# Splitting the K and V streams of a decode attention kernel over two DMA queues

## The chip, the cores and the metric

The kernel runs on one core of one Trainium2 chip. The metric is the device time of one execution in microseconds. A "span" is the time from the first to the last instruction in the profile of one execution; it is usually some 2 us less than the time. All ratios below are the mean time of one kernel's fast runs over that of the other's fast runs from the same rounds on the same chip, so they are not quite the ratio of the medians that are quoted.

## The reference, cut to what matters

Two independent problems, A and B, of one decode step of attention with a sliding window. Each has a batch of 2, 32 query heads, 16 key/value heads, and uses the last 4096 positions of a cache.

```python
q = (x @ wq).reshape(B, 1, 32, 128).transpose(0, 2, 1, 3)
k = jnp.repeat(k_cache[:, :, Sk - 4096:, :], 2, axis=1)
v = jnp.repeat(v_cache[:, :, Sk - 4096:, :], 2, axis=1)
p = softmax(jnp.einsum("bhqd,bhkd->bhqk", q, k) * 128 ** -0.5)
o = jnp.einsum("bhqk,bhkd->bhqd", p, v)
out = o.transpose(0, 2, 1, 3).reshape(B, 1, 4096) @ wo
# the results of A and B are concatenated
```

Nearly all of the work is to read K and V once: 2 problems x 16 heads x (K and V) x 2 MB, 134 MB, plus 19 MB of weights.

## The kernel before

A step t handles one "slab": the 4096 keys of one key/value head for both batch entries, 128 partitions x 8192 bf16, 2048 KB. There are 32 K slabs and 32 V slabs. PE is the matrix engine, DVE the vector engine and ACT the scalar engine; SP only issues transfers here. K and V slabs share a ring of eight slots. In step t the kernel

- transposes K(t) on DVE in two halves (X) and multiplies it with the query on PE (S);
- every fourth step, runs a softmax chain for four slabs: maximum on DVE, a few tiny matmuls, the bias copy and the exponentials on ACT, a transpose of the probabilities on DVE, the sum, and the copy of its reciprocal on ACT (rsb);
- multiplies the probabilities with V(t-5) on PE (PV), normalises the result on DVE, and every fourth step (in the last group every step) adds it into the output projection with wo.

K runs five steps ahead of V, since a chain needs the scores of four slabs. Each engine has a fixed list of operations in program order, and waits on semaphores for the others. The order of the loads is also a fixed list, all of it issued from the SP queue:

```python
stream = []
for t in range(NSLAB + LAG):               # NSLAB = 32, LAG = 5
    if t < NSLAB:
        stream.append(("K", t))
    if t >= LAG:
        i = t - LAG
        if i % 4 == 0:
            stream.append(("W", i // 4))   # a piece of wo
        stream.append(("V", i))
# ... slots are dealt out in this order, modulo 8 ...

def issue(key):
    # ... a slot's load waits for the last reader of what was in it:
    # K(t) for X(t-4), V(i) for PV(i-4); W(G) for the projection of group G-2
    stream_dma[key] = dma_op("sp", ring_sem[r], 1,
        lambda e: e.dma_start(ring[:, r, :], src).then_inc(ring_sem[r], 16), deps, "%s%d" % key)

def ensure(key):
    while key not in stream_dma:
        issue(stream[pos[0]])
        pos[0] += 1
```

K and V alternate in this list, so each already has four slots of the ring in the steady state: K the odd ones, V the even ones. At the end, with no K left, V(27), V(29) and V(31) go into slots that K had used. V(31) is loaded in two parts, three quarters and one quarter.

```python
for t in range(NSLAB + LAG + 1):
    i = t - LAG
    if t < NSLAB:
        make_X(t, 0); make_S(t, 0)         # calls ensure(("K", t))
    # ... if t % 4 == 0: first part of the softmax chain (the exponentials are on ACT)
    # ... norm and projection of V(i - 1)
    if t < NSLAB:
        make_X(t, 1); make_S(t, 1)
    # ... if t % 4 == 0: second part of the chain
    if 0 <= i < NSLAB:
        make_PV(i)                         # calls ensure(("V", i))
    # ... if t % 4 == 0: third part of the chain (rsb on ACT)
```

## Time and profile before

| | before |
|---|---|
| time, median of the first 3 runs | 370.98 us (370.94 to 371.55) |
| span of the profiled run | 369.0 us |
| DMA traffic | 153 MB, mean 416 GB/s |
| busy PE / DVE / ACT | 68% / 50% / 6% of the span |

First, lines of the profile's page. The rows "DMA" and "GB/s" cut the span into 40 equal slices; a digit is the mean busy share of the 16 DMA engines in tenths (9 is 90% or more). The q1 line is the SP queue: packets, MB, and the share of the 16 engines' time. The last line sums the chain of work that ended last by engine.

```profile
DMA  8999999999999999999999999999999999999992
GB/s 320 448 414 426 426 425 433 428 426 426 429 424 424 426 423 435 424 428 426 423 431 424 426 426 427 430 425 428 420 430 428 427 423 426 428 424 420 424 418 121
...
q1 hardware_dynamic: 11700, 153.10, 98.0%
...
DMA 87%; DVE 10%; PE 2%; SPq 1%; issue 0%
```

The DMA engines never rest between the first slice and the last one. At 426 GB/s a slab takes 4.9 us, and a K slab and a V slab together 9.8 us. The kernel is bound by the DMA stream.

From the same page, the DMA issues: tensor, queue, count, size of each, and the median time from issue to landing.

```profile
ring<-in_A_k_cache_dram SPq DMA_DIRECT2D x16, 2048.0 KB, 33.8
ring<-in_A_v_cache_dram SPq DMA_DIRECT2D x16, 2048.0 KB, 36.3
```

A slab lands 33 to 36 us after its issue although it only needs 4.9 us of transfer: about seven slabs are queued at any time.

Next, the start of the run in order of time, DVE alone: start, duration, line, operation, and in brackets the idle time before it and what ended it. "x2" merges the two halves of one K slab.

```profile
36.45 4.50 DVE L392 STREAM_TRANSPOSE xt<-ring 128x2048 f32<-128x2048 f32 x2 [0.39 <-DMA ring<-in_A_k_cache_dram]
41.33 4.50 DVE L392 STREAM_TRANSPOSE xt<-ring 128x2048 f32<-128x2048 f32 x2 [0.38 <-DMA ring<-in_A_k_cache_dram]
46.22 4.50 DVE L392 STREAM_TRANSPOSE xt<-ring 128x2048 f32<-128x2048 f32 x2 [0.38 <-DMA ring<-in_A_k_cache_dram]
51.11 2.31 DVE L392 STREAM_TRANSPOSE xt<-ring 128x2048 f32<-128x2048 f32 x1 [0.39 <-DMA ring<-in_A_k_cache_dram]
```

K(1) to K(4) arrive every 4.89 us: the queue moves nothing but K at first. Last, the end of the run: the first half of K(31) is transposed as soon as it lands, at 333.0; V(31) is issued (SPq is the SP queue); ACT computes rsb of the last chain; and PV(31) runs when V(31) has landed.

```profile
333.03 2.31 DVE L392 STREAM_TRANSPOSE xt<-ring 128x2048 f32<-128x2048 f32 x1 [5.22 <-DMA ring<-in_B_k_cache_dram]
...
340.55 0.61 SPq L340 DMA_DIRECT2D ring<-in_B_v_cache_dram  x1
...
351.21 0.19 ACT L498 ACTIVATE rsb<-tb 128x16 f32<-128x16 f32 x1 [4.01 <-PE tb L492]
...
364.21 2.05 PE L517 MATMUL ot<-pT,ring 128*128 128x56 bf16 x64 [0.16 <-DMA ring<-in_B_v_cache_dram]
```

After K(31) there are still 31 us of V transfers, and the last softmax chain hides behind them.

### The profile page before, as it was taken

How to read it: one execution, taken by the hardware profiler on the slowest of the kernel's cores; microseconds unless marked ns; L12 is line 12 of the kernel's file. 1: busy time of each engine (PE TensorE's matmuls, PEld its weight loads, DVE VectorE, ACT ScalarE, POOL GpSimd, SP SyncE). 2: the span in 40 equal slices, each digit the busy share in tenths (PEclk: the TensorE clock that was granted, in tenths of full speed). 3: DMA queues.
4: the chain of work that ended last, by engine and by line, in shares of the span. 5: the costliest groups of instructions: out<-in, count | busy, mean ns of one | idle time of the engine just before them, and what ended most of it. 6: DMA issues, size and time to landing. Idle time of an engine off the chain costs nothing.

```text
span 369.0 us, 6842 instructions
## 1 busy us (share of the span) xinstructions
PE 251.1 (68%) x3148; PEld 146.9 (40%) x3148; DVE 185.9 (50%) x213; ACT 23.0 (6%) x90; POOL 15.3 (4%) x49
## 2 busy tenths in 40 slices
PE   0648774956769758557769667666688667596666
PEld 0636232433436324333345334333255332362554
DVE  2105988543554465644655437364656444545310
ACT  1000002000200001000200002000200002000200
POOL 6010000000000000000000000000000000000000
PEclk9978999898589888998588888999578886996898
DMA  8999999999999999999999999999999999999992
GB/s 320 448 414 426 426 425 433 428 426 426 429 424 424 426 423 435 424 428 426 423 431 424 426 426 427 430 425 428 420 430 428 427 423 426 428 424 420 424 418 121
DMA packets 11740, 153.53 MB, mean 416 GB/s; under 512 B 1208, under 2 KB 2240, under 8 KB 2368
## 3 DMA queue, kind: packets, MB, share of 16 engines
q1 hardware_dynamic: 11700, 153.10, 98.0%
q8 instruction: 24, 0.39, 0.4%
q14 instruction: 4, 0.03, 0.0%
q10 hardware_dynamic: 12, 0.01, 0.0%
HBM read 153.10 MB, written 0.00 MB: 415 GB/s over the span
## 4 chain that ended last, share of the span: by engine, by line
DMA 87%; DVE 10%; PE 2%; SPq 1%; issue 0%
DMA ring<-in_B_k_cache_dram 41%; DMA ring<-in_A_k_cache_dram 40%; DVE xt L392 9%; DMA ring<-in_B_v_cache_dram 6%; PE st_0 L413 1%; PE ot L517 1%; SPq L348 0%; SPq L174 0%; DVE mx L422 0%; DVE oTg L532 0%; DVE out_sb L594 0%; PE pj L549 0%
## 5 line engine op out<-in xcount | busy, mean ns | idle before, releaser
L392 DVE STREAM_TRANSPOSE xt<-ring 128x2048 f32<-128x2048 f32 x64 | 146.0, 2292 | 100.7 <-DMA ring<-in_A_k_cache_dram 56.5
L413 PE MATMUL st_0<-xt,zq 128*128 128x512 bf16 x256 | 78.1, 457 | 53.4 <-DVE oTg L532 28.5
L413 PE MATMUL st_1<-xt,zq 128*128 128x512 bf16 x256 | 77.5, 454 | 30.6 <-DVE xt L392 30.6
L517 PEld LDWEIGHTS ot<-pT,ring 128*128 128x128 bf16 x2048 | 63.9, 100 | 13.2 <-DMA ring<-in_B_v_cache_dram 5.0
L517 PE MATMUL ot<-pT,ring 128*128 128x56 bf16 x2048 | 64.6, 193 | 3.8 <-DMA ring<-in_B_v_cache_dram 3.8
L413 PEld LDWEIGHTS st_0<-xt,zq 128*128 128x128 bf16 x256 | 25.1, 108 | 91.8 <-DVE oTg L532 30.7
L413 PEld LDWEIGHTS st_1<-xt,zq 128*128 128x128 bf16 x256 | 26.4, 110 | 73.0 <-DVE xt L392 36.8
L379 POOL TENSOR_TENSOR zq<-qs,bmask 128x64 bf16<-128x64 bf16 x32 | 9.3, 294 | 282.9 <-PE st_1 L413 267.8
L456 ACT ACTIVATE bias_sb<-tb 128x2 f32<-128x2 f32 x8 | 1.4, 172 | 249.5 <-PE tb L452 249.5
L256 PE MATMUL tb<-xU,ring 128*128 128x56 bf16 x288 | 11.8, 214 | 7.1 <-DMA ring<-in_B_wq_dram 5.2
L256 PEld LDWEIGHTS tb<-xU,ring 128*128 128x128 bf16 x288 | 11.5, 114 | 7.3 <-DMA ring<-in_B_wq_dram 5.4
L532 DVE TENSOR_TENSOR oTg<-ot,rsb 128x4 bf16<-128x4 f32 x32 | 4.3, 134 | 16.6 <-PE ot L517 16.5
L437 DVE TENSOR_REDUCE nM<-tb 1x8 f32<-1x64 f32 x16 | 2.7, 207 | 15.6 <-PE tb L428 15.6
L482 DVE STREAM_TRANSPOSE pT<-pR 128x512 bf16<-128x512 bf16 x16 | 10.4, 686 | 0.0
L452 PE MATMUL tb<-ones_f,nMrep 1*128 1x1 f32 x32 | 6.0, 288 | 6.0 <-DVE nMrep L446 6.0
L238 PE MATMUL tb<-ident_b,xt 2*128 2x2 bf16 x36 | 2.3, 194 | 10.3 <-DVE xt L208 10.3
L452 PEld LDWEIGHTS tb<-ones_f,nMrep 1*128 1x128 f32 x32 | 5.3, 234 | 9.2 <-DVE nMrep L446 9.2
L564 DVE TENSOR_TENSOR oM<-tb,hmask 128x128 f32<-128x128 f32 x7 | 2.0, 291 | 13.5 <-PE tb L560 13.5
L463 ACT ACTIVATE pR<-st_0,bias_sb 128x256 bf16<-128x256 f32 x16 | 8.2, 542 | 0.3
L463 ACT ACTIVATE pR<-st_1,bias_sb 128x256 bf16<-128x256 f32 x16 | 8.2, 548 | 0.0
L584 PE MATMUL pj<-wob,oP 128*2 128x288 bf16 x112 | 8.0, 285 | 0.0
L485 DVE TENSOR_REDUCE ssum<-tb 1x16 f32<-1x128 f32 x8 | 2.2, 273 | 9.6 <-PE tb L476 9.6
(48 smaller groups left out, 72.3 us busy)
## 6 DMA issues: line engine op xcount, KB each, us to landing
ring<-in_A_k_cache_dram SPq DMA_DIRECT2D x16, 2048.0 KB, 33.8
ring<-in_A_v_cache_dram SPq DMA_DIRECT2D x16, 2048.0 KB, 36.3
ring<-in_B_k_cache_dram SPq DMA_DIRECT2D x16, 2048.0 KB, 34.9
ring<-in_B_v_cache_dram SPq DMA_DIRECT2D x15, 2048.0 KB, 33.2
ring<-in_A_wq_dram SPq DMA_DIRECT2D x1, 4608.0 KB, 13.7
ring<-in_B_wq_dram SPq DMA_DIRECT2D x1, 4608.0 KB, 25.4
wob<-in_A_wo_dram SPq DMA_DIRECT2D x4, 1152.0 KB, 29.4
wob<-in_B_wo_dram SPq DMA_DIRECT2D x4, 1152.0 KB, 28.4
```

The source lines that it names most:

```text
L238: last = e.transpose(bb[0:128, o:o + Bb], src, ident_b[0:Bb, 0:Bb])
L256: last = e.matmul(bank[:, c * 64:c * 64 + NS], wqv[P][:, u, cb * 128:(cb + 1) * 128], xU[:, P, u, 0:NS], start=(u == 0), stop=(u == NU - 1))
L379: return e.tensor_tensor(dst, src, msk, ALU.mult)
L392: Xop[(t, jb)] = S.add("dve", lambda e: e.transpose(xt[:, n % NXT, :].bitcast(FP32), ring[:, r, jb * HW_:(jb + 1) * HW_].bitcast(FP32)), d ...
L413: last = e.matmul(st[:, 0:512], zq[:, p4, m, 16 - 16 * jl:144 - 16 * jl], mv, start=(m == 0 and jl == 0 and p4 == 0), stop=True, skip_grou ...
L437: last = e.tensor_reduce(dst, src, AX.X, ALU.max, negate=True)
L452: last = e.matmul(bank[:, t:t + 1], nMrep[0:1, t, :], ones_f[0:1, 0:1], start=True, stop=True)
L463: last = e.activation(pR[:, jb, :].rearrange("p (x t) -> p t x", t=2)[:, t, :], st[jb][:, :].rearrange("p (x t) -> p t x", t=2)[:, t, :], ...
L482: chain[(G, "pT%d" % jb)] = S.add("dve", lambda e, jb=jb: e.transpose(pT[:, v, 512 * jb:512 * jb + 512], pR[:, jb, :]), deps, "pT%d_%d" % ...
L517: last = e.matmul(ot[:, 0:NS], ring[:, r, j * 128:(j + 1) * 128], pT[:, v, col:col + NS], start=(j == 0), stop=(j == KR - 1))
L532: norm_op[i] = S.add("dve", lambda e: e.tensor_tensor(oTg[:, v, 2 * m:2 * m + 2, :], OT[i % 2][:, 0:4].rearrange("d (b h) -> d h b", h=2), ...
L584: last = e.matmul(PJ[half], oP[:, v, j, :], wob[:, v, j, half * NH:(half + 1) * NH], start=(proj_start(G) and j == 0), stop=True, skip_gro ...
```

## The change

The intent is to have two independent load streams. V slabs are issued from the ACT queue, V(i) at the start of step i+2, three steps before its use; K slabs and wo stay on SP. A wait of a K load then no longer blocks a V load, and SP saves the issue time of 33 DMAs. Slots, sizes and the waits of each load stay as they are.

```diff
@@ issue
             P, g = i // Hkv, i % Hkv
+            q = "sp" if kind == "K" else "act"
 ...
-            stream_dma[key] = dma_op("sp", ring_sem[r], 1,
+            stream_dma[key] = dma_op(q, ring_sem[r], 1,
                 (the two parts of V(31) likewise)
 
+        sp_stream = [key for key in stream if key[0] != "V"]
+
         def ensure(key):
+            if key[0] == "V":
+                assert key in stream_dma
+                return
             while key not in stream_dma:
-                issue(stream[pos[0]])
+                issue(sp_stream[pos[0]])
                 pos[0] += 1
@@ make_proj_direct and make_proj
+            ensure(("W", G))
@@ the main loop
         for t in range(NSLAB + LAG + 1):
             i = t - LAG
+            if 0 <= t - 2 < NSLAB:
+                issue(("V", t - 2))
```

More of the change, by code (lines that the diff above doesn't have):

```diff
@@ L343, in fb @@
                     return e.dma_start(ring[:, r, last_split:SW], s0[:, :, cut:KR, :].rearrange("r b j d -> r b (j d)")).then_inc(last_sem, 16)
-                stream_dma[key] = dma_op("sp", ring_sem[r], 1, fa, deps, "%s%da" % key)
-                stream_dma[("tail", 0)] = dma_op("sp", last_sem, 1, fb, deps, "%s%db" % key)
+                stream_dma[key] = dma_op(q, ring_sem[r], 1, fa, deps, "%s%da" % key)
+                stream_dma[("tail", 0)] = dma_op(q, last_sem, 1, fb, deps, "%s%db" % key)
                 return
-            stream_dma[key] = dma_op("sp", ring_sem[r], 1,
+            stream_dma[key] = dma_op(q, ring_sem[r], 1,
                                      lambda e: e.dma_start(ring[:, r, :], src).then_inc(ring_sem[r], 16), deps, "%s%d" % key)
+        sp_stream = [key for key in stream if key[0] != "V"]
         def ensure(key):
+            if key[0] == "V":
+                assert key in stream_dma
+                return
             while key not in stream_dma:
-                issue(stream[pos[0]])
+                issue(sp_stream[pos[0]])
                 pos[0] += 1
@@ L586, in f @@
                 return last
+            ensure(("W", G))
             deps = [chain[(G, "oP")], stream_dma[("W", G)]]
```

## The prediction

> **What bounds the kernel now.** The page's slice row shows the 16 DMA engines 90% busy or more in every slice but the first and last, at 414 to 448 GB/s; the queue table gives the one SP queue 98.0% of their time for 153 MB. The chain that ended last is 87% DMA and 10% DVE transposes. PE is busy 68%, DVE 50%, ACT 6%. A 2,048 KB slab therefore costs about 4.9 us, and a step (one K slab, one V slab) 9.8 us. A DMA takes 33 to 36 us from issue to landing (issue table): seven slabs are queued at any time, so the waits that I find on the SP queue (146 us for the K transposes, 47 us for the P·V matmuls, 41 us for the projection) starve nothing. The Trainium skill, "DMA: Bandwidth & Descriptors", Specifications, gives a fabric ceiling of 435 GB/s; the slices' 425 or so agree, and leave at most 2%.
>
> **What the change does.** No byte, no slot and no dependency changes. 33 DMA issues (0.54 us each on SP) move to ACT, which is 6% busy. V(i) is still gated by P·V(i-4), K(t) by the transpose of K(t-4). The same skill page ("Issuing engines are not separate DMA queues") says that both queues run on the same 16 engines and that this saves only issue time; under "Queues, rings and completion order" it says that each engine takes turns between queues packet by packet. The trace of before, with one loaded queue, cannot show either. So I expect no gain in the middle: still about 425 GB/s, engines 90% busy.
>
> What moves is the order of arrival. Before, the queue's order lets K run ahead: K(31) landed at 333.0 us (timeline), with 31.2 us of DMA, about 6.3 slabs, after it, and that V data hid the last softmax chain. After, V takes half the bandwidth as soon as its slot is free. wo loads cost only the K queue, so V drifts ahead until its four slots limit it. Start: V(0) to V(2) are fetched beside K(1) to K(4), so K(4) lands some 15 us later than its 51.1 us; the work is only reordered.
>
> **Tail.** K(31) will land later, estimated at 338 to 347 us, with 3.5 to 5 slabs left. Also V(31) now stands on ACT behind the last chain's rsb activation, which waits for P·V(27). In the timeline rsb ran at 351.2, 18.2 us after K(31) landed; before, V(31) had been issued at 340.6. Thus V(31) would be issued 16 to 18 us after K(31) (later if DVE has a backlog), need about 7 us to land (4.9 us plus start), and 4.8 us of final P·V, projection and store follow: K(31) + about 30 us. Before, that path would have ended near 363 against the 369.0 of the DMA stream: some 5 us of slack. With K(31) 5 to 14 us later the slack goes, and a DMA gap of 0 to 8 us opens ahead of V(31). I take 4 us.
>
> **Time.** 371.0 + 4 = 375.0 us, range 369.5 to 380. Faster by over 2%: 3%; within 2%: 79%; slower by over 2%: 18%.
>
> **What would show it.** Middle slices unchanged; two DMA queues, about 69 MB on ACT's and 84 MB on SP's; first K transposes spread out; K(31) later than 333 us; rsb then V(31)'s issue then its landing on the final chain; a DMA gap just before it. Engine waits grow off the critical path only.
>
> **What would make it wrong.** Two interleaved streams may change DMA efficiency by a per cent or two either way; the shares may not be equal, so V does not get ahead and no gap opens (time stays at 371); or V gets so far ahead that K starves mid-run and the gap is nearer 10 us.

## The result, and the profile after

| | before | after |
|---|---|---|
| time, median of 6 runs (range) | 371.3 us (370.94 to 372.68) | 378.1 us (376.83 to 378.74) |
| ratio | 1 | 1.017, 95% interval 1.0143 to 1.0197 |
| span of the profiled run | 369.0 us | 376.6 us |
| K(31) landed | 333.0 us | 347.1 us |
| DMA rate from 36 to 320 us | 426 GB/s | 427 GB/s |

The change costs 1.7%, 7 us. The page's lines again; q10 is the ACT queue.

```profile
DMA  8999999999999999999999999999999999999833
GB/s 322 431 428 428 430 426 432 426 430 423 421 431 425 426 433 420 429 426 428 428 422 430 425 428 423 428 425 432 424 426 426 429 424 428 424 432 421 361 111 146
...
q1 hardware_dynamic: 6948, 85.99, 54.0%
q10 hardware_dynamic: 4764, 67.12, 42.2%
...
DMA 76%; PE 11%; DVE 11%; ACT 1%; issue 0%; SPq 0%
```

Up to the 37th slice the two kernels move bytes equally fast. The difference is the end: in the last three slices the rate falls to 361, 111 and 146 GB/s. The windows view of one stretch puts numbers on it (the length, the busy time of each engine with its count, then the granted PE clock, the DMA share, and GB/s). Before:

```profile
core 0: us, PE busy (x) PEld busy (x) DVE busy (x) ACT busy (x) POOL busy (x), PEclk, DMA share, GB/s
36.00:320.00 284.00, 200.95 (x2191) 108.72 (x2191) 161.07 (x180) 17.14 (x71) 8.22 (x28) 0.85 1.01 426
...
355.00:365.00 10.00, 6.25 (x158) 5.13 (x159) 0.32 (x2) 0.00 (x0) 0.00 (x0) 0.83 0.74 308
```

After:

```profile
36.00:320.00 284.00, 186.79 (x2103) 100.04 (x2104) 155.33 (x169) 16.94 (x70) 8.22 (x28) 0.88 1.01 427
...
355.00:365.00 10.00, 6.73 (x131) 6.17 (x128) 3.20 (x13) 2.39 (x10) 0.00 (x0) 0.66 0.30 105
```

The DMA engines are busy 30% of the ten microseconds from 355 on, against 74% before: the gap that the prediction spoke of. The issues show who is now ahead:

```profile
ring<-in_A_k_cache_dram SPq DMA_DIRECT2D x16, 2048.0 KB, 34.3
ring<-in_A_v_cache_dram ACTq DMA_DIRECT2D x16, 2048.0 KB, 16.3
```

A V slab lands 16 us after its issue, a K slab still 34 us: V has a short queue of its own and takes half of the engines as soon as a slot is free. The start of the run on DVE shows the sharing directly:

```profile
36.42 4.51 DVE L398 STREAM_TRANSPOSE xt<-ring 128x2048 f32<-128x2048 f32 x2 [0.46 <-DMA ring<-in_A_k_cache_dram]
46.20 4.50 DVE L398 STREAM_TRANSPOSE xt<-ring 128x2048 f32<-128x2048 f32 x2 [5.28 <-DMA ring<-in_A_k_cache_dram]
55.99 4.50 DVE L398 STREAM_TRANSPOSE xt<-ring 128x2048 f32<-128x2048 f32 x2 [5.28 <-DMA ring<-in_A_k_cache_dram]
65.78 2.31 DVE L398 STREAM_TRANSPOSE xt<-ring 128x2048 f32<-128x2048 f32 x1 [5.29 <-DMA ring<-in_A_k_cache_dram]
```

K(1) to K(4) now arrive every 9.78 us, twice the 4.89 us of before. The end in order of time (ACTq is the ACT queue):

```profile
347.11 2.31 DVE L398 STREAM_TRANSPOSE xt<-ring 128x2048 f32<-128x2048 f32 x1 [5.22 <-DMA ring<-in_B_k_cache_dram]
...
363.32 0.18 ACT L504 ACTIVATE rsb<-tb 128x16 f32<-128x16 f32 x1 [4.17 <-PE tb L498]
363.33 0.54 ACTq L341 DMA_DIRECT2D ring<-in_B_v_cache_dram  x1
...
371.95 1.89 PE L523 MATMUL ot<-pT,ring 128*128 128x56 bf16 x64
```

K(31) lands 14.1 us later than before, V(31) is issued right behind rsb, and PV(31) starts at 371.95. Which of the two late things holds up the end? The chain that ended last, in order of time (start, duration, what; merged):

```profile
309.69 37.40 DMA ring<-in_B_k_cache_dram
...
347.11 2.31 DVE xt L398
...
357.12 2.04 ACT pR L469 x8
...
359.77 2.99 PE ot L523 x64
...
367.17 1.77 PE ot L523 x64
...
372.01 1.84 PE ot L523 x64
...
374.54 0.45 DVE out_sb L602
```

It runs from the landing of K(31) through the last softmax chain and the last P·V products to the output, 29.5 us of compute, without touching the load of V(31). But V(31) landed at nearly the same time: by the DMA view its first part took 7.1 us from its issue at 363.3, and its second 7.9 us from 363.9, so it was there at about 371.8, and PV(31) began at 372.0. The profile alone cannot say which of the two costs the 7 us. So there were three theories:

1. Arrival order. Fair sharing lets V get ahead of K; K(31) lands late, and the compute after it no longer hides under V transfers.
2. Issue position. V(31) stands behind rsb in ACT's program order, and its late issue opens the DMA gap.
3. Two queues cost bandwidth as such.

### The profile page after: what moved, and what is told of

It reads as the page before. It is cut to its first block, busy times and chain, and to the rows that moved or that the text cites. A ratio compares the mean times of both kernels' runs of the same rounds, so it can differ in the third digit from the quotient of the medians.

```text
span 376.6 us, 6840 instructions
## 1 busy us (share of the span) xinstructions
PE 244.5 (65%) x3148; PEld 143.0 (38%) x3148; DVE 185.4 (49%) x213; ACT 23.0 (6%) x90; POOL 15.3 (4%) x49
## 4 chain that ended last, share of the span: by engine, by line
DMA 76%; PE 11%; DVE 11%; ACT 1%; issue 0%; SPq 0%
DMA ring<-in_B_k_cache_dram 40%; DMA ring<-in_A_k_cache_dram 32%; DVE xt L398 10%; PE ot L523 4%; DMA ring<-in_A_wq_dram 4%; PE st_1 L419 2%; PE st_0 L419 2%; PE tb L256 2%; ACT pR L469 1%; PE pj L555 0%; SPq L349 0%; DVE oTg L538 0%; PE pj L591 0%; PE tb L458 0%; DVE nM L443 0%
## 5 line engine op out<-in xcount | busy, mean ns | idle before, releaser
L419 PE MATMUL st_0<-xt,zq 128*128 128x512 bf16 x256 | 78.1, 457 | 69.0 <-DVE oTg L538 46.0
L419 PE MATMUL st_1<-xt,zq 128*128 128x512 bf16 x256 | 74.9, 442 | 33.1 <-DVE xt L398 33.1
L523 PEld LDWEIGHTS ot<-pT,ring 128*128 128x128 bf16 x2048 | 62.1, 99 | 8.3 <-issue 3.1
L523 PE MATMUL ot<-pT,ring 128*128 128x56 bf16 x2048 | 62.8, 191 | 0.0
L458 PE MATMUL tb<-ones_f,nMrep 1*128 1x1 f32 x32 | 4.8, 250 | 6.0 <-DVE nMrep L452 6.0
L458 PEld LDWEIGHTS tb<-ones_f,nMrep 1*128 1x128 f32 x32 | 4.1, 185 | 8.6 <-DVE nMrep L452 8.6
L428 DVE TENSOR_REDUCE mx<-st_1 128x2 f32<-128x512 f32 x8 | 5.4, 677 | 1.4 <-PE st_1 L419 1.4
```

Of the source, the lines that this page charges most:

```text
L419: last = e.matmul(st[:, 0:512], zq[:, p4, m, 16 - 16 * jl:144 - 16 * jl], mv, start=(m == 0 and jl == 0 and p4 == 0), stop=True, skip_grou ...
L428: mxs = [S.add("dve", lambda e, jb=jb: e.tensor_reduce(mx[:, jb, :], st[jb][:, :].rearrange("p (x t) -> p t x", t=2), AX.X, ALU.max), [Sop ...
L458: last = e.matmul(bank[:, t:t + 1], nMrep[0:1, t, :], ones_f[0:1, 0:1], start=True, stop=True)
L523: last = e.matmul(ot[:, 0:NS], ring[:, r, j * 128:(j + 1) * 128], pT[:, v, col:col + NS], start=(j == 0), stop=(j == KR - 1))
```

## The experiments

No experiment takes a wait away; each load still waits for the last reader of its slot. All kernels gave correct results. Landings and spans are those of the one run of each kernel that was profiled. Every kernel ran for five rounds, one_ahead for three; a single figure in brackets after a time is the number of runs.

### v31_early: the changed kernel with V(31) issued before the last chain

```diff
-            if 0 <= t - 2 < NSLAB:
+            if 0 <= t - 2 < NSLAB - 1:
                 issue(("V", t - 2))
+            if t == NSLAB:
+                issue(("V", NSLAB - 1))
```

Expected:

> The changed kernel, with V(31) issued on ACT before the last softmax chain instead of after its rsb activation (no wait removed: the slot's last reader is still waited for). Theory 1, arrival order: K(31) lands late (347 us) because V takes half the bandwidth, and the work after it (transpose, scores, chain, four P.V products, projection, store) takes 29.5 us of compute that no longer hides under V loads; V(31)'s place does not matter, time stays at 377 to 378.5 us, the DMA gap before V(31) vanishes. Theory 2, issue position: V(31) waiting behind rsb on ACT opens the gap and costs the 7 us; time goes back to 371 to 373 us. Theory 3, two queues as such cost bandwidth over the whole run: no change, 378 us, but the middle slices stay below those of before.

Measured: 377.54 us (5), ratio to before 1.0177 (1.0155 to 1.0198); the changed kernel had 1.017. The page's DMA row and five lines of the end (the second but last is the first matmul with the last piece of wo):

```profile
DMA  8999999999999999999999999999999999999960
```

```profile
340.30 0.54 ACTq L341 DMA_DIRECT2D ring<-in_B_v_cache_dram  x1
...
344.09 2.31 DVE L398 STREAM_TRANSPOSE xt<-ring 128x2048 f32<-128x2048 f32 x1 [3.82 <-DMA ring<-in_B_k_cache_dram]
...
361.04 0.18 ACT L504 ACTIVATE rsb<-tb 128x16 f32<-128x16 f32 x1 [3.75 <-PE tb L498]
...
365.57 0.41 PE L555 MATMUL pj<-wob,oTg 128*2 128x288 bf16 x4 [1.53 <-DMA wob<-in_B_wo_dram]
...
370.76 1.83 PE L523 MATMUL ot<-pT,ring 128*128 128x56 bf16 x64
```

V(31) is issued 23 us earlier, the gap is gone (the row is full until the last two slices), and the time is the same. K(31) landed at 344.1 in this run, 3 us earlier than in the changed kernel's, and the span ended 31.3 us later, against 29.5 there. Of these 31.3 us, 1.5 are a new wait, for the last piece of wo: it was issued at 339.0 us and landed 26.5 us later, while the V slabs moved in the other queue. The chain that ended last runs through this load and not through K(31):

```profile
338.96 26.48 DMA wob<-in_B_wo_dram
```

Without that wait the span would have been about 373.9 us (an estimate: 375.4 less 1.5), still some 5 us over the 369.0 of before, and K(31) plus 29.8. So taking away the late issue of V(31), and the DMA gap with it, won nothing here. Theory 2 falls as the main cause; since the landings of K(31) and wo moved too, a small share of it is not excluded by this run.

### one_queue_late1, 2 and 3: the kernel before with K(31) later in its one queue

```diff
+        stream.remove(("K", NSLAB - 1))
+        stream.remove(("W", NG - 1))
+        at = stream.index(("V", NSLAB - 4)) + 1      # late3; NSLAB - 5 in late2, NSLAB - 6 in late1
+        stream[at:at] = [("K", NSLAB - 1)]
+        at = max(at + 1, stream.index(("V", NSLAB - 5)) + 1)
+        stream[at:at] = [("W", NG - 1)]
         stream_dma = {}
@@ make_proj_direct
+            ensure(("W", G))
```

The slots are dealt out before this, so they do not change. In late3 the last piece of wo moves behind V(28) too, so that it stays behind K(31). Expected, in the order in which they ran:

> The kernel before, one SP queue, with K(31) moved three V slabs later in that queue (behind V(28)), so that it lands near 347.7 us instead of 333.0, as in the changed kernel. V(31) is issued early from SP. Theory 1: same loss without any second queue: compute ends 29.5 to 31 us after K(31), 377 to 380.5 us. Theory 2 and theory 3: no second queue and no late V(31), so 371 us.

> The kernel before with K(31) one V slab later in the one queue: it lands near 338 us. Theory 1: compute ends 29.5 to 31 us later, 367.5 to 369, about where the DMA stream ends anyway: the slack is just used up, 371 to 372 us, within 0.3% of before.

> The kernel before with K(31) two V slabs later: it lands near 343 us. Theory 1: 343 + 30.8 + 2 = 375.5 us (374.5 to 376.5), so 1.0 to 1.4% slower: each slab past the slack costs its full 4.9 us. If the loss of one_queue_late3 came from something else than K(31)'s landing (the moved wo load, say), no such step is seen.

Measured:

| | K(31) landed | span | from K(31) to the end | time (median, runs) | ratio to before (95%) |
|---|---|---|---|---|---|
| before | 333.0 | 369.0 | 36.0 | 371.02 (11) | 1 |
| one_queue_late1 | 338.1 | 368.9 | 30.8 | 371.00 (6) | 0.9995 (0.997 to 1.002) |
| one_queue_late2 | 342.9 | 373.3 | 30.4 | 375.28 (6) | 1.0101 (1.0081 to 1.012) |
| one_queue_late3 | 347.8 | 378.6 | 30.8 | 380.56 (4) | 1.0248 (1.0232 to 1.0263) |

(The 371.02 us are of the rounds of late1 and late2; in the rounds of late3, before took 371.18 us.) The landings are read from the idle time that ends with the transpose of K(31), one line from each timeline:

```profile
338.08 2.31 DVE L398 STREAM_TRANSPOSE xt<-ring 128x2048 f32<-128x2048 f32 x1 [10.12 <-DMA ring<-in_B_k_cache_dram]
```

```profile
342.93 2.31 DVE L398 STREAM_TRANSPOSE xt<-ring 128x2048 f32<-128x2048 f32 x1 [15.07 <-DMA ring<-in_B_k_cache_dram]
```

```profile
347.79 2.31 DVE L398 STREAM_TRANSPOSE xt<-ring 128x2048 f32<-128x2048 f32 x1 [19.55 <-DMA ring<-in_B_k_cache_dram]
```

One queue, no V load on ACT, the same bytes, V(31) issued by 346 us at the latest; and the loss appears with the landing of K(31) alone. The chains that ended last agree: that of late1 ends through the load of V(31), those of late2 and late3 run from the landing of K(31) through compute to the end. The first slab of delay is free: it uses up the slack. Each further slab costs about its full 4.9 us. The end is the later of 369.0 (the DMA stream) and K(31) plus 30.8. Put 347.1, the landing in the changed kernel, into this rule, and it gives a span of 377.9 where 376.6 was measured. That is theory 1, and the size is right to 1.3 us.

### hold and hold_early: V(27) to V(30) wait for K(31)

```diff
+            if kind == "V" and NSLAB - 5 <= i < NSLAB - 1:
+                ensure(("K", NSLAB - 1))
+                deps = deps + [stream_dma[("K", NSLAB - 1)]]
             if key == stream[-1]:
```

hold_early adds the edit of v31_early.

> The changed kernel, with V(27) to V(30) issued only after K(31) has landed; V(31) stays behind rsb. Only the last 50 us differ. Theory 1: K(31) lands near 337 us instead of 347, compute ends by about 367, the DMA stream is the last again: 371 to 373 us. Theory 2: V(31) is still issued 16 us after K(31); the V slabs queued at K(31) now fill that time, so it also allows 371 to 373; it differs from theory 1 by v31_early alone. Theory 3: no better than 377.

> Both edits: V(27) to V(30) wait for K(31), and V(31) is issued before the last chain. Theory 1: as hold, 371 to 372.5 us, the early issue adds less than 1 us. Theory 2: 371. Theory 3: 377 or more.

Measured: hold 1.0064 (1.0045 to 1.0084), from its three fast runs of 373.22 to 374.14 us; hold_early 1.0079 (1.0056 to 1.0103), from four fast runs of 373.01 to 375.36 us. The other three runs of hold and two of hold_early took 382 to 384 us and count as slow; no ratio is read from them, and why they differ was not found. The kept profile of hold is of such a run: in it the last piece of wo was issued 2.6 us after V(27) to V(30), landed 27.9 us later and held PE up for 6.0 us. In the profiled run of hold_early, a fast one, it was issued 1.6 us before them and landed in 5.8 us. Whether this is what parts the slow runs from the fast ones was not tested. In the fast runs most of the loss is gone, but the times are a little over what was expected. The page of hold_early (a fast run) shows a new gap:

```profile
GB/s 318 444 416 432 425 435 425 425 433 421 427 428 423 428 426 422 432 425 423 430 423 427 426 433 421 425 432 427 421 432 423 423 434 425 425 382 277 433 422 161
```

The slice with 277 GB/s, from 335 to 344 us, is where V(27) was held back until all of K(31) had landed, while the queue had nothing else to move but, from 336.6 on, a piece of wo. As a way to order two streams the wait for a landing was poor here: the queues ran nearly dry before it could end.

### tail_sp and tail_sp_wo: only the last five V slabs back on SP

```diff
-            q = "sp" if kind == "K" else "act"
+            q = "sp" if kind == "K" or i >= NSLAB - 5 else "act"
 ...
-        sp_stream = [key for key in stream if key[0] != "V"]
+        sp_stream = [key for key in stream if key[0] != "V" or key[1] >= NSLAB - 5]
 ...
-            if key[0] == "V":
+            if key[0] == "V" and key[1] < NSLAB - 5:
 ...
-            if 0 <= t - 2 < NSLAB:
+            if 0 <= t - 2 < NSLAB - 5:
```

> The changed kernel, with only V(27) to V(31) taken back to the SP queue, behind K(31), in the order of the kernel before; V(0) to V(26) stay on ACT, and no transfer waits for another to land, unlike in hold, whose wait for K(31) let the queue run dry. Theory 1, arrival order at the end: K(31) lands near 336 to 340 us, no DMA gap, the last V slab lands last: 371 to 372.5 us; the whole loss undone by the last five V slabs. If part of the loss sits in the first 320 us (theory 3), the time stays at 374 or more.

Measured: 373.54 us (6 runs, 371.02 to 375.18), ratio 1.0051 (1.0015 to 1.0086). Two thirds of the loss are gone, but not all, so the expectation of 371 to 372.5 was missed. The waits of the SP queue between 318 and 345 us suggest a reason:

```profile
SPq L321 <- PE pj L591: 17.4, 1, 17.4
```

SP stood 17.4 us before the last wo load, waiting for a projection, with V(28) to V(31) behind it; from 335 to 340 us the DMA engines were 75% busy. In the kernel before the same wait exists (15.7 us) but ends earlier, at 326 us. tail_sp_wo therefore moves that load behind V(29):

```diff
+        stream.remove(("W", NG - 1))
+        stream.insert(stream.index(("V", NSLAB - 3)) + 1, ("W", NG - 1))
         stream_dma = {}
```

> tail_sp, with the last wo load moved behind V(29) in the SP queue. In tail_sp the profile shows SP waiting for a projection until 339.4 us before that wo load, with V(28) to V(31) behind it, and the DMA engines 75% busy from 335 to 340 us. If that wait is what is left of the loss (0.5%), the queue no longer runs dry and the time is 371 to 372 us, the ratio within 0.3% of 1. If the remainder comes from two queues over the first 320 us, it stays at 373.5.

Measured: 372.04 us (6 runs, 370.82 to 374.3), ratio 1.0011 (0.9985 to 1.0036). The DMA engines stay over 90% busy from 318 to 359 us. With 27 of the 32 V slabs still on the ACT queue, the time is that of before within the noise (at most 0.4% by the interval): theory 3 falls, and within that noise the loss is undone by the order of the last loads. That it was the moved wo load that brought the step from tail_sp is not shown: the two intervals overlap, and the two profiled runs have the same span, 372.2 and 372.3 us. What is left is an uneven scatter of 3.5 us. The profile fell on the slowest of these runs, 374.3 us, and its chain runs on compute alone from the landing of K(28) to the end (so does that of tail_sp, whose profile is also of its slowest run, from 312.95 us; the wo load that SP waited for is not on it):

```profile
277.81 35.26 DMA ring<-in_B_k_cache_dram
...
313.08 2.32 DVE xt L400
...
370.23 0.45 DVE out_sb L604
```

K(28) landed at 313.1 here, against 300.9 before (both read from the transpose): sharing up to that point had already delayed it, and 57 us of compute from there to the output copy leave no slack. Why other runs of this kernel were 3 us faster was not settled.

### one_ahead: V issued one step ahead instead of three

```diff
-            if 0 <= t - 2 < NSLAB:
-                issue(("V", t - 2))
+            if 0 <= t - 4 < NSLAB:
+                issue(("V", t - 4))
```

> The changed kernel with each V slab issued from ACT one step ahead of its use instead of three. ACT has no other work in three steps of four, so only the last softmax chain should matter: V(29) to V(31), three slabs, now stand behind its rsb activation. K(31) lands earlier than in the changed kernel (about 340 us), then the queue runs dry until rsb some 16 us later, then three slabs need about 17 us and the end 5 us: 378 to 386 us. If ACT's program order does not matter even here, the time is that of before or of the changed kernel, 371 to 378.

Measured: 377.48 us (4), ratio 1.0148 (1.0117 to 1.018), just under the expected range and, by the number alone, inside that of the other outcome (371 to 378); the profile tells them apart. The end:

```profile
334.63 2.31 DVE L398 STREAM_TRANSPOSE xt<-ring 128x2048 f32<-128x2048 f32 x1 [4.21 <-DMA ring<-in_B_k_cache_dram]
...
351.65 0.18 ACT L504 ACTIVATE rsb<-tb 128x16 f32<-128x16 f32 x1 [4.17 <-PE tb L498]
...
360.05 3.06 PE L523 MATMUL ot<-pT,ring 128*128 128x56 bf16 x64 [4.42 <-DMA ring<-in_B_v_cache_dram]
...
369.63 2.53 PE L523 MATMUL ot<-pT,ring 128*128 128x56 bf16 x64 [2.19 <-DMA ring<-in_B_v_cache_dram]
```

Here K(31) lands at 334.6, early enough by the rule above (365.4), yet the kernel is as slow as the changed one, for the other reason: V(29) to V(31) stand behind rsb at 351.65, and the last products wait for their loads (4.42 us and 2.19 us of idle PE in the lines above). So theory 2's mechanism is real and binds where three slabs are affected; in the changed kernel, with one slab, it came out level with the compute path. I had expected K(31) at 340; it came at 334.6, probably because V with less lead takes less of the engines before the end; this was not tested.

## Why the prediction was right or wrong

The time was forecast as 375.0 (369.5 to 380) and measured as 378.1. The direction was right, and somewhat more than half of the size (4 us of some 7).

- "So I expect no gain in the middle": right. 426 against 427 GB/s over 284 us. What the Trainium skill says in "DMA: Bandwidth & Descriptors", section "Issuing engines are not separate DMA queues", namely that the queues share the same 16 engines and a second one saves only issue time, agrees with this trace.
- "each engine takes turns between queues": right. The skill's section "Queues, rings and completion order" says that engines go round the queues that have work, packet by packet; the spacing of K slabs going from 4.89 to 9.78 us is an even split. K(4) was forecast "some 15 us later than its 51.1 us" and came at 65.8.
- "V drifts ahead until its four slots limit it": supported by the V landings of 16 us against 34 us for K; the drift itself was not measured step by step.
- "K(31) ... estimated at 338 to 347 us": 347.1, the very end of the range.
- "a DMA gap of 0 to 8 us opens ahead of V(31). I take 4 us": the step that failed. Taken as a size, it was the middle of a range whose upper end came true: span plus 7.6 us. Taken as a mechanism, the gap is there but is not the cost: with the gap closed (v31_early) the time did not change, though 1.5 us of a wait for wo came in. The term that counts is the landing of K(31) plus its compute. The prediction had the sum nearly right, "K(31) + about 30 us" against 29.5 measured, but explained those 30 us by rsb, the issue of V(31), its landing and the last product. In fact two paths of equal length leave K(31): that one, and the pure compute path through the last chain and four P·V products with their projections. The chain after shows the second. That they are equally long was luck, and it is why the sum came out.
- "some 5 us of slack": right in size, by the same luck, since it was worked out for the path through V(31) and the runs show it for the compute path. One slab of 4.9 us was free, the second cost 4.3 us (375.28 against 371.00), the third 5.3 us.
- "rsb then V(31)'s issue then its landing on the final chain": wrong, for the reason above.

## What to carry to other kernels

When a kernel is bound by one deep queue, moving a stream to a second queue need not add bandwidth (here 427 GB/s against 426); it turned "first in, first out" into "share and share alike", and so changed which data arrived last. Ask what compute follows the last piece of each stream, and keep the stream with the longest tail of compute in front: here one slab of slack was free and each slab beyond it cost about its full transfer time. Look at the small loads in these queues too: in v31_early it was the last piece of wo, and neither K nor V, that the end waited for. No version tried beat the kernel before.

## What the Trainium skill lacked or had wrong

- "DMA: Bandwidth & Descriptors", "Rules for kernel authors": the row on spreading DMAs over several issuing engines says that it does not help. It lacks that it can hurt: two queues of 2 MB slabs shared the engines evenly, where one kept the order, and that change of arrival order cost 1.7% here (K slabs every 9.78 us instead of every 4.89; one_queue_late3 makes a loss of the same kind, 2.5%, with one queue). Nor was the sharing even for every load: the last piece of wo, 1152 KB in pieces of 1152 bytes, took 26.5 us beside V slabs in v31_early.
- The same page, "Where 436 GB/s comes from": it says that for transfers between HBM and SBUF the HBM side, about 358 GB/s, binds; one core read 426 GB/s over 284 us here. The page's section "Bandwidth" sets this right itself: about 358 GB/s is for each of two cores of one HBM domain that stream at once, and a single core reached 425 GB/s. The row in "Specifications" lacks that condition.
- No page that I read gives a time by which the 16 engines finish apart after a long stream. In the kernel before, the DMA share falls from 96% (357 to 359 us) over 81% and 55% to 39% (363 to 365 us); in hold_early, with K(31) not yet landed and nothing else queued, it was 67% and 46% from 332 to 336 us, and K(31) landed at 338. These are means over the 16 engines; that some finish later than others is inferred from them and not shown engine by engine.
